# LayerNorm's reciprocal square root moved from GpSimd to VectorE, in a two-layer decode kernel

## The chip, the cores and the metric

The kernel runs on one core of a Trainium2 chip. The metric is the device time of one execution in microseconds; lower is better. The core has TensorE (matrix products, PE in the profile), VectorE (DVE), ScalarE (ACT), GpSimd (POOL) and SyncE (SP), which here issues the transfers. All of them run their own queue of instructions in order and wait for one another by semaphores.

## What is computed

Two decoder layers for eight sequences (B = 8) with one new token each, with the same weights and caches in both layers. Each layer is an attention block and a small MLP, both behind a LayerNorm without scale or offset:

```python
def _layernorm(x, axis=-1, eps=1e-5):
    m = jnp.mean(x, axis=axis, keepdims=True)
    v = jnp.var(x, axis=axis, keepdims=True)
    return (x - m) / jnp.sqrt(v + eps)

    # _A_ref: B=8, Sq=1, D=512, Hq=32, Hkv=8, Sk=8192, Dh=128
    q = (x @ wq) ...                                   # 512 -> 32 heads of 128
    scores = einsum("bhqd,bhkd->bhqk", q, k) * (Dh ** -0.5)
    o = einsum("bhqk,bhkd->bhqd", softmax(scores), v)
    return o ... @ wo                                  # 4096 -> 512
    # _B_ref: F=1792
    return silu(x @ w1) @ w2

    x = A_x
    x = x + _A_ref(_layernorm(x), A_k_cache, A_v_cache, A_wq, A_wo)
    x = x + _B_ref(_layernorm(x), B_w1, B_w2)
    x = x + _A_ref(_layernorm(x), A_k_cache, A_v_cache, A_wq, A_wo)
    x = x + _B_ref(_layernorm(x), B_w1, B_w2)
```

The K and V caches are 8 x 8 x 8192 x 128 bf16 each, and both layers read all of both, so the kernel is mostly a stream of these caches through the core.

## The kernel before

**Tasks and positions.** A task is one layer, one batch row and one KV head: 128 tasks (`make_tasks`). A task is cut into eight positions; each position is half of a granule of 512 KB, eight chunks of 128 keys. At a position TensorE transposes the eight chunks of K (`emit_t`, L383, three positions ahead), a copy on VectorE or ScalarE brings the result back from PSUM (L391, L389), TensorE makes the scores (`emit_s`, L414) and, twelve positions later, multiplies P by V (`emit_pv`, L464). Softmax of a task takes its four steps at the first four positions of the next task: a maximum on VectorE (L423) and across partitions on GpSimd (L425), the subtraction on VectorE (L432) and the exponential on ScalarE (L439), a sum on VectorE (L444) and across partitions on GpSimd (L447), the reciprocal (L452). `emit_norm` (L478) finishes the head.

**Loads.** SyncE issues all transfers (L296), in an order planned beforehand (`plan_loads`), into an arena of 27 slots of 512 KB. A slot is loaded anew when the products that read it are done. Eighteen granules of K of each batch row stay in their slots from the first layer to the second, so that their K is loaded and transposed once; the other nine slots carry the stream.

**The order of tasks.** For each batch row b: the kept heads of layer 0, then three heads of layer 1 of row b - 1, then three heads of layer 0 of row b + 1, then the kept heads of layer 1 of row b.

**The chain.** Between layer 0's attention of a batch row and its layer 1 stands a chain of twelve stages (`chain_of`): `proj` (output projection and residual), three LayerNorm stages `first`, `second`, `third`, `up`, `silu`, `down`, the three LayerNorm stages again, and `query`. One stage is taken out of the list at each position, behind that position's other work, while the tasks of the neighbouring rows go on. Every engine executes in the order of issue, so where TensorE comes to the project of `up` or `query` (L523) it waits for `xnT`, the normalized row, and what was issued behind it waits too. The whole batch goes through one LayerNorm and `query` at the start, and through one `block_stages` at the end, on eight columns instead of one.

**LayerNorm** (`ln_stages`). x lies transposed, 128 partitions x 4 x n columns. `first`: a sum on VectorE into `s1` (L486) and across partitions on GpSimd into `s1a` (L488). `second`: centring into `xc` (L494), square (L500), sum (L501) on VectorE, the partition sum on GpSimd (L503), then on GpSimd the scaling by 1/D with epsilon (L505) and the power of -0.5 (L507), against a tile `nhalf` that is filled once (L327). `third`: the product of `xc` and `s1a` on VectorE into `xnT` (L511). Each call of `op` makes the instruction wait for the last writers of what it reads and for the readers of what it writes, on the same engine too.

## Time and profile before

| | |
|---|---|
| median of 3 runs | 1486.3 us (1485.43 to 1490.5) |
| the profiled execution: its own time | 1487.09 us |
| its span, first to last instruction | 1485.4 us |
| mean granted TensorE clock | 0.71 |
| instructions in the trace | 56919 |
| read from HBM | 473.44 MB, 319 GB/s over the span |
| GpSimd busy | 134.1 us, 338 instructions |
| VectorE busy | 511.5 us, 1246 instructions |

The profile describes one execution. A line of its groups gives source line, engine, operation, output and input tiles, number of instructions, then busy time and the mean of one, and behind the bar the idle time of the engine just before them with what ended it. "issue" means that the engine waited for nothing that the profile shows. POOLq and SPq are the sequencers of GpSimd and SyncE; an instruction that only they execute does not count as busy time. The row named DMA gives for 40 equal slices of the span the busy share of the 16 DMA engines in tenths. Windows repeat the busy times for chosen stretches, with the granted clock, the share of the DMA engines and GB/s at the end of each line.

### The profile page before, as it was taken

What the parts mean: (1) busy time and instruction counts of PE and PEld (TensorE: products, weight loads), DVE (VectorE), ACT (ScalarE), POOL (GpSimd) and SP (SyncE); (2) the same over time, 40 slices, a digit from 0 to 9 for tenths busy, and PEclk for the clock granted to TensorE, in tenths of its full rate; (3) what the DMA queues carried; (4) which work ended last, traced back from release to release, by engine and by line L of the source; (5) the groups of instructions that cost most, each with busy time, mean ns of one, the idle gap of its engine ahead of it and who ended that gap; (6) DMA issues with size and microseconds to landing.
All of it is one profiled execution on the core that took longest, in us unless ns stands there. A gap on an engine that the chain in (4) does not pass through costs nothing.

```text
span 1485.4 us, 56919 instructions
## 1 busy us (share of the span) xinstructions
PE 1008.5 (68%) x25592; PEld 982.2 (66%) x25592; DVE 511.5 (34%) x1246; ACT 327.6 (22%) x414; POOL 134.1 (9%) x338
## 2 busy tenths in 40 slices
PE   2777478658776677856687476783868667775674
PEld 2777477657776567756687476773867667775663
DVE  1343134324342334423344133431434324342331
ACT  1232013212231212312133121330313212231210
POOL 0100010010000110000100001000100011000011
PEclk6788568757696767856588575975868756796665
DMA  8999399829996599956999569993999839996591
GB/s 352 381 407 366 115 403 408 326 102 402 407 405 251 196 408 407 394 188 240 406 407 387 182 263 407 408 355 133 353 408 407 312 130 402 408 388 259 203 408 66
DMA packets 133984, 477.13 MB, mean 321 GB/s; under 512 B 14176, under 2 KB 20080, under 8 KB 133232
## 3 DMA queue, kind: packets, MB, share of 16 engines
q1 hardware_dynamic: 133744, 473.51, 82.2%
q8 instruction: 203, 3.33, 0.9%
q14 instruction: 37, 0.30, 0.1%
HBM read 473.44 MB, written 0.01 MB: 319 GB/s over the span
## 4 chain that ended last, share of the span: by engine, by line
PE 45%; issue 27%; DMA 22%; DVE 3%; POOL 2%; SPq 1%; POOLq 0%; ACT 0%; DVEq 0%
PE TPp L383 20%; DMA arena<-in_A_k_cache_dram 18%; PE SCp L414 10%; PE OTp L464 9%; PE MISC L523 5%; DMA arena<-in_A_v_cache_dram 3%; DVE arena L391 1%; POOL s1a L507 1%; DMA wq<-in_A_wq_dram 1%; SPq L296 1%; POOL s1a L503 0%; POOL mxa L425 0%; POOL s1a L505 0%; DVE sq L500 0%; DVE s L501 0%
## 5 line engine op out<-in xcount | busy, mean ns | idle before, releaser
L383 PE MATMUL TPp<-ident,arena 128*128 128x128 bf16 x5888 | 561.5, 252 | 102.3 <-DMA arena<-in_A_k_cache_dram 69.6
L383 PEld LDWEIGHTS TPp<-ident,arena 128*128 128x128 bf16 x5888 | 422.7, 113 | 110.4 <-DMA arena<-in_A_k_cache_dram 77.1
L391 DVE COPY arena<-TPp 128x1024 bf16<-128x1024 bf16 x460 | 317.2, 690 | 433.0 <-PE TPp L383 430.3
L389 ACT COPY arena<-TPp 128x1024 bf16<-128x1024 bf16 x276 | 278.6, 1009 | 739.4 <-PE TPp L383 739.3
L414 PE MATMUL SCp<-QT,arena 128*128 128x32 bf16 x8192 | 394.4, 184 | 66.7 <-issue 64.0
L464 PE MATMUL OTp<-P,arena 128*128 128x4 bf16 x8192 | 360.8, 165 | 81.6 <-issue 73.4
L414 PEld LDWEIGHTS SCp<-QT,arena 128*128 128x128 bf16 x8192 | 338.7, 103 | 67.8 <-issue 64.2
L464 PEld LDWEIGHTS OTp<-P,arena 128*128 128x128 bf16 x8192 | 290.9, 100 | 95.2 <-issue 86.2
L439 ACT ACTIVATE P<-SCs 128x256 bf16<-128x256 f32 x128 | 53.4, 417 | 384.6 <-DVE SCs L432 331.5
L425 POOL PARTITION_ALL_REDUCE mxa<-mxp x128 | 47.7, 373 | 738.6 <-DVE mxp L423 666.9
L523 PE MATMUL MISC<-xnT,wq 128*128 128x1 bf16 (+1 forms) x1152 | 32.1, 165 | 92.0 <-DVE xnT L511 92.0
L523 PEld LDWEIGHTS MISC<-xnT,wq 128*128 128x128 bf16 x1152 | 31.4, 104 | 92.7 <-DVE xnT L511 77.3
L432 DVE TENSOR_TENSOR SCs<-SCp,mxa 128x256 f32<-128x256 f32 x128 | 53.9, 421 | 87.2 <-POOL mxa L425 87.2
L447 POOL PARTITION_ALL_REDUCE ssa<-ssm x128 | 55.1, 430 | 265.7 <-DVE ssm L444 253.9
L523 PE MATMUL MISC<-xnT,w 128*128 128x1 bf16 (+1 forms) x504 | 14.9, 166 | 86.2 <-DVE xnT L511 86.2
L523 PEld LDWEIGHTS MISC<-xnT,w 128*128 128x128 bf16 x504 | 14.2, 104 | 86.9 <-DVE xnT L511 80.1
L423 DVE TENSOR_REDUCE mxp<-SCp 128x4 f32<-128x256 f32 x128 | 53.4, 417 | 44.5 <-PE SCp L414 44.5
L511 DVE TENSOR_TENSOR xnT<-xc,s1a 128x4 bf16<-128x4 f32 (+1 forms) x18 | 3.2, 178 | 187.3 <-POOL s1a L507 187.3
L444 DVE TENSOR_REDUCE ssm<-P 128x4 f32<-128x256 bf16 x128 | 53.3, 416 | 41.4 <-ACT P L439 41.4
L478 DVE TENSOR_TENSOR at<-OTp,rcp 128x4 bf16<-128x4 f32 x128 | 20.0, 156 | 61.0 <-PE OTp L464 61.0
L523 PE MATMUL MISC<-at,wo 128*128 128x1 bf16 (+1 forms) x1152 | 32.5, 165 | 12.5 <-issue 12.2
L523 PEld LDWEIGHTS MISC<-at,wo 128*128 128x128 bf16 x1152 | 31.3, 101 | 13.2 <-issue 12.8
(33 smaller groups left out, 111.7 us busy)
## 6 DMA issues: line engine op xcount, KB each, us to landing
arena<-in_A_v_cache_dram SPq DMA_DIRECT2D x512, 512.0 KB, 10.1
arena<-in_A_k_cache_dram SPq DMA_DIRECT2D x368, 512.0 KB, 11.8
wq<-in_A_wq_dram SPq DMA_DIRECT2D x2, 2048.0 KB, 9.3
wo<-in_A_wo_dram SPq DMA_DIRECT2D x1, 4096.0 KB, 27.7
w<-in_B_w_dram SPq DMA_DIRECT2D x2, 1792.0 KB, 23.4
X<-in_A_x_dram SPq DMA_DIRECT2D x1, 8.0 KB
out_dram<-X SPq DMA_DIRECT2D x1, 8.0 KB
```

What stands on the lines that cost most here:

```text
L383: lambda c=c: pe.transpose(tpv[:, c, :], chunk(slot, h * GRP + c), ident[:, :])
L389: op(act, lambda: act.copy(dst, TPp[tb][:, :]), reads=[f"TP{tb}"], writes=[r_half(slot, h)])
L391: op(dve, lambda: dve.tensor_copy(dst, TPp[tb][:, :]), reads=[f"TP{tb}"], writes=[r_half(slot, h)])
L414: lambda c=c, o=o: pe.matmul(SCp[bank][:, o:o + SW], chunk(slot, h * GRP + c), rhs, start=True, stop=True,)
L423: op(dve, lambda: dve.tensor_reduce(mxp[st][:, :], scv, AX.X, ALU.max), reads=[f"SC{bank}"], writes=[f"mxp{st}"])
L425: op(pool, lambda: pool.partition_all_reduce(mxa[st][:, :], mxp[st][:, :], 128, bass.bass_isa.ReduceOp.max), reads=[f"mxp{st}"], writes=[f ...
L432: lambda: dve.tensor_tensor(SCs[:, :].rearrange("p (c h) -> p c h", h=REP), SCp[bank][:, 0:NCH * REP].rearrange("p (c h) -> p c h", h=REP) ...
L439: op(act, lambda: act.activation(Ps[pb][:, :], SCs[:, :], ACT.Exp, scale=SM_SCALE), reads=["SCs"], writes=[f"P{pb}"])
L444: op(dve, lambda: dve.tensor_reduce(ssm[st][:, :], Ps[pb][:, :].rearrange("p (c h) -> p h c", h=REP), AX.X, ALU.add), reads=[f"P{pb}"], wr ...
L447: op(pool, lambda: pool.partition_all_reduce(ssa[st][:, :], ssm[st][:, :], 128, bass.bass_isa.ReduceOp.add), reads=[f"ssm{st}"], writes=[f ...
L464: lambda c=c, cc=cc: pe.matmul(otp, chunk(slot, h * GRP + c), Ps[pb][:, cc * REP:(cc + 1) * REP], start=(cc == 0), stop=(cc == NCH - 1),)
L523: lambda o=o, k=k: pe.matmul(MISC[:, o * n:(o + 1) * n], w_sb[:, k, o * 128:(o + 1) * 128], rhs_of(k), start=(k == 0), stop=(k == kparts - 1),
```

## The change

The two GpSimd operations behind the second partition sum and the tile `nhalf` go. `third` computes 1/sqrt(v) on VectorE instead, ahead of the product: v = s1a/D + eps into a tile `vr`; a first guess y from the bits of v, read as an integer (shift right by one, times -1, plus the constant 0x5F3759DF); three Newton steps y = y (1.5 - 0.5 v y y), each in three operations over the tiles `tr` and `yr`. That is twelve operations on n columns. GpSimd keeps the memsets and the mask at the start, and the partition sums and maxima.

```diff
+RSQRT_SEED = float(0x5F3759DF)
+NEWTON = 3
...
-    nhalf = sb([128, B], FP32, "nhalf")
+    vr = sb([128, B], FP32, "vr")
+    yr = sb([128, B], FP32, "yr")
+    tr = sb([128, B], FP32, "tr")
...
-            op(pool, lambda: pool.memset(nhalf[:, :], -0.5), writes=["nhalf"])
...
                     op(pool, lambda: pool.partition_all_reduce(s1a[:, 0:n], s1[:, 0:n], 128, bass.bass_isa.ReduceOp.add),
                        reads=["s1"], writes=["s1a"])
-                    op(pool, lambda: pool.tensor_scalar(s1a[:, 0:n], s1a[:, 0:n], 1.0 / D, LN_EPS, op0=ALU.mult, op1=ALU.add),
-                       reads=["s1a"], writes=["s1a"])
-                    op(pool, lambda: pool.tensor_tensor(s1a[:, 0:n], s1a[:, 0:n], nhalf[:, 0:n], ALU.pow),
-                       reads=["s1a", "nhalf"], writes=["s1a"])
-
                 def third():
+                    v, y, t = vr[:, 0:n], yr[:, 0:n], tr[:, 0:n]
+                    vi, yi = v.bitcast(INT32), y.bitcast(INT32)
+                    op(dve, lambda: dve.tensor_scalar(v, s1a[:, 0:n], 1.0 / D, LN_EPS, op0=ALU.mult, op1=ALU.add),
+                       reads=["s1a"], writes=["vr"])
+                    op(dve, lambda: dve.tensor_scalar(yi, vi, 1, None, op0=ALU.logical_shift_right),
+                       reads=["vr"], writes=["yr"])
+                    op(dve, lambda: dve.tensor_scalar(yi, yi, -1.0, RSQRT_SEED, op0=ALU.mult, op1=ALU.add),
+                       reads=["yr"], writes=["yr"])
+                    for _n in range(NEWTON):
+                        op(dve, lambda: dve.tensor_tensor(t, y, y, ALU.mult), reads=["yr"], writes=["tr"])
+                        op(dve, lambda: dve.scalar_tensor_tensor(t, t, -0.5, v, op0=ALU.mult, op1=ALU.mult),
+                           reads=["tr", "vr"], writes=["tr"])
+                        op(dve, lambda: dve.scalar_tensor_tensor(y, t, 1.5, y, op0=ALU.add, op1=ALU.mult),
+                           reads=["tr", "yr"], writes=["yr"])
                     op(dve, lambda: dve.tensor_tensor(
-                        xnv, xcv, s1a[:, 0:n].unsqueeze(1).to_broadcast([128, KT, n]), ALU.mult),
-                       reads=["xc", "s1a"], writes=["xnT"])
+                        xnv, xcv, y.unsqueeze(1).to_broadcast([128, KT, n]), ALU.mult),
+                       reads=["xc", "yr"], writes=["xnT"])
```

More of the change, by code (lines that the diff above doesn't have):

```diff
@@ L27 @@
 FP32 = mybir.dt.float32
+INT32 = mybir.dt.int32
 ACT = mybir.ActivationFunctionType
```

## The prediction, made before the changed kernel ran

> **What bounds the kernel now.** I read the page first, then the waits, then the two GpSimd lines by source, then one stretch in order of time, and the same stretch in windows. From the page:

> ```profile
> PE 1008.5 (68%) x25592; PEld 982.2 (66%) x25592; DVE 511.5 (34%) x1246; ACT 327.6 (22%) x414; POOL 134.1 (9%) x338
> ...
> DMA  8999399829996599956999569993999839996591
> ...
> L511 DVE TENSOR_TENSOR xnT<-xc,s1a 128x4 bf16<-128x4 f32 (+1 forms) x18 | 3.2, 178 | 187.3 <-POOL s1a L507 187.3
> ```

> No compute engine is full (PE busy 68% of the span, the others less), while most slices of the DMA row stand at 9: there the loads of K and V set the pace, at 405 to 410 GB/s by the windows. The eight dips are the matter. Adding up, over windows of 10 us, what each falls short of 408 GB/s gives 310 us of lost transfer time: 262 in the dips (32.8 each), 26 after the last load, 5 at the start, the rest scattered. The dips are the eight chains (`proj`, LayerNorm, MLP, LayerNorm, `query`), one per batch row. The third line says what happens there: VectorE waits 187.3 us for the power on GpSimd, in 18 LayerNorms. The waits name the next in line and the source:

> ```profile
> PE MISC L523 <- DVE xnT L511: 178.2, 18, 15.4
> ...
> POOL s1a L505 <- issue: 173.5, 18, 10.9
> ...
> POOL mxa L425 <- issue: 71.7, 12, 6.3
> ...
> PE MISC L523 <- DVE hsT L557: 32.9, 9, 4.0
> ```

> (Columns: total us, times, longest.) TensorE stands behind `xnT` for 178.2 us. GpSimd itself waits for nothing that the profile shows ("issue"), 173.5 us ahead of L505. The lines by source show an instruction that the program does not write:

> ```profile
> L505 POOLq MODIFY_POOL_CONFIG  x36: 83/83/88, 27.3 to 1467.5; - x36
> ```
> ```profile
> L425 POOLq MODIFY_POOL_CONFIG  x34: 11/11/11, 40.4 to 1390.2; - x34
> ```

> Two for each of the 18 LayerNorms where GpSimd goes from a partition reduction to ordinary arithmetic, and two for each of 17 ways back. The 256 softmax reductions that follow one another carry none. So it is the alternation that costs, some 10 us out and 6 us back. One chain, in order of time (start, duration, engine, line; in brackets idle time before and its releaser):

> ```profile
> 643.79 0.17 DVE L500 TENSOR_TENSOR sq<-xc 128x4 f32<-128x4 f32 x1
> 643.99 0.16 DVE L501 TENSOR_REDUCE s<-sq 128x1 f32<-128x4 f32 x1
> ...
> 644.25 0.39 POOL L503 PARTITION_ALL_REDUCE s1a<-s  x1 [1.29 <-DVE s L501]
> ...
> 654.42 0.18 POOL L505 TENSOR_SCALAR s1a<-s1a 128x1 f32<-128x1 f32 x1 [9.79 <-issue]
> 654.68 0.60 POOL L507 TENSOR_TENSOR s1a<-s1a,nhalf 128x1 f32<-128x1 f32 x1
> 655.31 0.18 DVE L511 TENSOR_TENSOR xnT<-xc,s1a 128x4 bf16<-128x4 f32 x1 [10.83 <-POOL s1a L507]
> ...
> 655.54 1.65 PE L523 MATMUL MISC<-xnT,w 128*128 128x1 bf16 x56 [9.96 <-DVE xnT L511]
> ...
> 661.22 0.39 POOL L425 PARTITION_ALL_REDUCE mxa<-mxp  x1 [5.94 <-issue]
> ...
> 663.65 1.65 PE L523 MATMUL MISC<-hsT,w 128*128 128x1 bf16 x56 [3.90 <-DVE hsT L557]
> ```

> In windows of the same stretch (PE, PEld, DVE, ACT, POOL busy; then clock, DMA share, GB/s):

> ```profile
> 650.00:660.00 10.00, 4.21 (x104) 4.13 (x104) 0.77 (x2) 0.00 (x0) 0.78 (x2) 0.50 0.05 20
> ...
> 670.00:680.00 10.00, 0.00 (x0) 0.00 (x0) 0.00 (x0) 0.00 (x0) 0.78 (x2) 0.60 0.48 183
> ...
> 690.00:700.00 10.00, 7.72 (x198) 7.37 (x196) 5.08 (x12) 3.34 (x4) 0.80 (x2) 0.97 1.00 379
> ```

> With TensorE standing, no arena slot comes free, the loads in flight run out, and transfers stop: 20 GB/s. Ten microseconds of GpSimd become lost load time.

> **The change, part by part.** *Removed: two GpSimd operations, and with them the alternation.* [...] `up` waits now 86.2 us in nine, of which 11.5 in the tail: 74.7/8 = 9.34 a chain. `query` waits 92.0 in nine, 15.4 at the start: 76.6/8 = 9.58.

> *Added: twelve VectorE operations ahead of `xnT`,* each on one column (eight at both ends of the kernel). None of them is in this trace. The nearest rows are sq and s above: 0.17 and 0.16 us, 0.20 from start to start, each waiting for the one before, as the new ones do. The bounds are 0.155 (the shortest mean of a small VectorE row) and 0.31 (the reciprocal, L556). I take 0.20, since the tiles are as small as those of the nearest rows: 12 x 0.20 = 2.4 us. They begin when the second reduction ends, at 644.64; `xnT` is there at 644.7 + 2.4 + 0.18 = 647.3, and TensorE, which had ended its groups at 645.58, waits 1.8. In `query` a VectorE copy ends first, at 669.39: 669.39 + 2.4 + 0.25 = 672.0 against 669.97, a wait of 2.05. So per chain 9.34 - 1.8 + 9.58 - 2.05 = 15.1 us less. Queued behind the twelve on VectorE are the copies of transposed K, the subtraction and the sums of softmax; TensorE would need them only after the project that it is waiting to start, so they add nothing of their own.

> *The way back goes too.* At 661.22 a softmax maximum waited for GpSimd; behind it in order stood the subtraction on VectorE, then its exponential and the MLP's on ScalarE, then `hsT`, and `down` on TensorE. Of 32.9 us, 1.9 are the tail: 31.0/8 = 3.88 a chain. Without it `up` ends at 647.33 + 1.65 = 648.98, the exponential and three VectorE operations (0.18 + 0.20 + 0.34 + 0.18) give `hsT` by 649.9, and TensorE comes to `down` two positions of 1.28 later, 651.5. I take 0 left. Sum: 15.1 + 3.88 = 18.95 us per chain, and 8 x 18.95 = 151.6. Does a microsecond of TensorE bring one of the end? The dip loses 32.8 us of transfers, more than what is given back, and both sides of it run at the full rate; so yes.

> *What comes to light.* In the busy stretches TensorE stops by itself: between 718 and 818 us its "issue" gaps end 6.1 to 6.7 us apart, 126 matmuls each. With every gap the instruction queue moves one 16 KB packet. `query` alone has 128 matmuls, issued in 3.57 us; today the wait ahead of it hides that. If the next packet comes late, a gap like the 2.24 us in `proj` (ended at 639.91) appears: at most 8 x 2.24 = 18 us, at least 0. Transfers are thin there, so I take 5.

> *The ends.* In the last LayerNorm nothing lies beside the chain: from the end of the reduction (1467.54) to `xnT` (1476.58) 9.04 us; afterwards 12 x 0.23, the pitch of the eight-column rows there, and 0.05: 2.8. Gain 6.2. At the start the first `xnT` comes some 10 us earlier, but transfers then run at 407 GB/s until 50 us; only 2.3 us are missing between 50 and 70, so 0 to 2.3, taken as 1. The dropped memset runs at 0.8 us, beside the load of x: nothing.

> The profiled execution took 1487.1 us (span 1485.4), 0.8 above the median. 1487.1 - 151.6 - 6.2 - 1 + 5 = 1333; on the median, 1332.

> [...] Going to ordinary arithmetic took 9.8 to 10.9 us in the chains and 7.0 in the tail, with no transfers about. [...]

> A second row concerns the short waits that remain:

> ```profile
> 756.82 0.61 PE L383 MATMUL TPp<-ident,arena 128*128 128x128 bf16 x8
> ...
> 761.71 1.01 PE L383 MATMUL TPp<-ident,arena 128*128 128x128 bf16 x8
> ```

> Between them TensorE stood for 2.20 us, and the granted clock fell from 1.00 to 0.50 for the next 5.3. After a gap of 1.88 (at 753.0) it stayed at 1.00, after one of 1.85 (at 772.8) it fell to 0.51. So waits of 1.8 and 2.05 may go either way; I keep positions in the chain at 1.28 us, as now. Were the clock up for six of them, at 0.85 us, 6 x 0.43 x 8 = 21 us more would be won.
> [...]

> **The rivals.** [...] 4%. [...]
> *The loads hide it:* only the tail is won, 1481. Against: transfers are at 20 GB/s in the wait itself. 2%.
> *TensorE's instructions become the bound:* two gaps of 2.24 us a chain instead of the 5 us in all: 1333 - 5 + 36 = 1364. The regular gaps speak for it, the thin transfers against. 14%.
> *The clock stays up:* 1333 - 21 = 1312. 14%.
> *The whole dip closes:* 1487 - 262 - 6 = 1219. Against: a chain's own 368 matmuls still take 10.4 us. 3%.

> **How the numbers follow.** The forecast keeps 63%. VectorE's pitch moves it by 16 x 12 x (-0.045 to +0.11) = -9 to +21, gaps by -5 to +13, the clock by -21, the start by 1: 1297 to 1368. I give 1297 to 1370, which takes in the third and fourth rivals. About 0.3%, 4.5 us, is what a measurement can tell from no change: faster 0.95, same 0.01, slower 0.04.

> **What would show it.** MODIFY_POOL_CONFIG only at the start; no "issue" ahead of L425; TensorE's waits for `xnT` near 40 us instead of 178, for `hsT` under 5; dips of some 14 us instead of 32.8; VectorE up by 216 operations and about 35 us. It is wrong if the dips keep their depth, if the twelve take over 4 us, or if new "issue" gaps stand in `query`.

## The result, and the profile after

The changed kernel takes 1329.1 us (median of four, 1323.6 to 1332.0) against 1485.9 before: a ratio of 0.894, 95% interval 0.890 to 0.897, 156.8 us less. The forecast was 1332, between 1297 and 1370. On another chip the same kernel gave 1328.8 us and 0.893 (0.890 to 0.896). The profiled execution took 1323.6 us (span 1321.8), the fastest of its four; with the 1487.1 of before, the two profiles are 163.5 us apart, and the sums below go by that.

In the page of the changed kernel VectorE has 216 instructions more and 34 us more of work, GpSimd 37 fewer, and the row of transfers has lost its deep dips:

```profile
PE 1009.8 (76%) x25592; PEld 983.4 (74%) x25592; DVE 545.3 (41%) x1462; ACT 328.8 (25%) x414; POOL 117.8 (9%) x301
...
DMA  8999899969999799997999889997999979999892
```

In full windows of 10 us, what is missing from 408 GB/s adds up to 150.6 us instead of 310.6. Each of the eight dips now loses some 15 us of transfers, against some 34 before when both are counted by the windows under 398 GB/s. Its waits (total us, times, longest) answer those of before line by line:

```profile
DVE SCs L436 <- POOL mxa L429: 39.7, 80, 0.5
...
PE MISC L536 <- DVE xnT L524: 36.6, 18, 5.0
...
PE MISC L536 <- issue: 13.2, 9, 2.5
...
PE MISC L536 <- DVE hsT L570: 1.9, 1, 1.9
```

TensorE waits 36.6 us for `xnT` (178.2 before) and 1.9 for `hsT` (32.9 before), while its wait for K from memory stays (70.8 us, 69.6 before) and its own work too (1009.8 us busy, 1008.5 before); "issue" ahead of a partition reduction is gone, and no wait of the subtraction for a maximum is longer than 0.5 us (6.2 before). By source, MODIFY_POOL_CONFIG is left at two places, both in the first 10 us (before the mask and before the first reduction, where the kernel before has it too), and in no chain:

```profile
L335 POOLq MODIFY_POOL_CONFIG  x2: 11/11/11, 1.0 to 1.0; - x2
```
```profile
L492 POOLq MODIFY_POOL_CONFIG  x2: 1/1/1, 9.9 to 9.9; - x2
```

One chain in order of time, to be laid beside that of the prediction:

```profile
588.80 0.40 POOL L507 PARTITION_ALL_REDUCE s1a<-s  x1 [1.28 <-DVE s L505]
...
589.13 0.42 POOL L429 PARTITION_ALL_REDUCE mxa<-mxp  x1
589.23 0.15 DVE L512 TENSOR_SCALAR vr<-s1a 128x1 f32<-128x1 f32 x1 [0.19 <-POOL s1a L507]
589.42 0.15 DVE L514 TENSOR_SCALAR yr<-vr 128x1 int32<-128x1 int32 x1
...
591.35 0.16 DVE L522 SCALAR_TENSOR_TENSOR yr<-tr,yr 128x1 f32<-128x1 f32 x1
591.54 0.18 DVE L524 TENSOR_TENSOR xnT<-xc,yr 128x4 bf16<-128x4 f32 x1
...
591.77 1.62 PE L536 MATMUL MISC<-xnT,w 128*128 128x1 bf16 x56 [1.75 <-DVE xnT L524]
...
595.82 1.63 PE L536 MATMUL MISC<-hsT,w 128*128 128x1 bf16 x56
...
604.07 3.45 PE L536 MATMUL MISC<-xnT,wq 128*128 128x1 bf16 x128 [1.50 <-DVE xnT L524]
```

From the end of the second reduction to `xnT` it is 2.3 us, where it was 10.7. The softmax maximum follows the reduction at once, `down` has no wait left, and from the project of `up` to that of `query` it is 12.3 us, where it was 24.7.

### The profile page after: what moved, and what is told of

It is laid out like the page before. It is cut to its first block, busy times and chain, and to the rows that moved or that the text cites. A ratio compares the mean times of both kernels' runs of the same rounds, so it can differ in the third digit from the quotient of the medians.

```text
span 1321.8 us, 57028 instructions
## 1 busy us (share of the span) xinstructions
PE 1009.8 (76%) x25592; PEld 983.4 (74%) x25592; DVE 545.3 (41%) x1462; ACT 328.8 (25%) x414; POOL 117.8 (9%) x301
## 4 chain that ended last, share of the span: by engine, by line
PE 53%; DMA 23%; issue 17%; DVE 5%; SPq 1%; POOL 1%; ACT 0%; POOLq 0%; DVEq 0%; ACTq 0%
PE TPp L387 24%; DMA arena<-in_A_k_cache_dram 18%; PE SCp L418 12%; PE OTp L468 11%; PE MISC L536 7%; DMA arena<-in_A_v_cache_dram 3%; SPq L301 1%; DVE arena L395 1%; DMA wq<-in_A_wq_dram 1%; DVE yr L522 1%; DVE tr L520 1%; DVE tr L519 1%; POOL s1a L507 0%; DVE xnT L524 0%; DVE yr L514 0%
## 5 line engine op out<-in xcount | busy, mean ns | idle before, releaser
L387 PE MATMUL TPp<-ident,arena 128*128 128x128 bf16 x5888 | 564.0, 253 | 109.2 <-DMA arena<-in_A_k_cache_dram 70.8
L456 DVE RECIPROCAL rcp<-ssa 128x4 f32<-128x4 f32 x128 | 22.0, 172 | 22.8 <-POOL ssa L451 22.8
L536 PE MATMUL MISC<-xnT,w 128*128 128x1 bf16 (+1 forms) x504 | 14.6, 165 | 18.4 <-DVE xnT L524 18.4
```

What stands on the lines that cost most here:

```text
L387: lambda c=c: pe.transpose(tpv[:, c, :], chunk(slot, h * GRP + c), ident[:, :])
L536: lambda o=o, k=k: pe.matmul(MISC[:, o * n:(o + 1) * n], w_sb[:, k, o * 128:(o + 1) * 128], rhs_of(k), start=(k == 0), stop=(k == kparts - 1),
```

## The experiments

The theory of the prediction: GpSimd's change between partition reductions and ordinary arithmetic (the exchange, below) is what costs; it stops TensorE, and so the loads; the twelve VectorE operations cost what they lengthen TensorE's wait. Rivals: that the power itself was slow; that only the reader of `s1a` suffers; that VectorE's work is hidden, or costs by its place in VectorE's queue. Ratios are to the kernel before on the same chip.

**One scaling back on GpSimd.** The eleven other operations stay on VectorE and read `s1a`.

```diff
 # end of second()
+op(pool, lambda: pool.tensor_scalar(s1a[:, 0:n], s1a[:, 0:n], 1.0 / D, LN_EPS, op0=ALU.mult, op1=ALU.add), ...)
 # start of third()
-op(dve, lambda: dve.tensor_scalar(v, s1a[:, 0:n], 1.0 / D, LN_EPS, op0=ALU.mult, op1=ALU.add), ...)
```

> The scaling by 1/D with epsilon goes back to GpSimd, right behind the second partition sum; the other eleven VectorE operations stay, the power is gone. [...] Against the kernel before, eleven operations at 0.195 us (2.15) stand where the power and its gap (0.66) stood, 1.5 us in each of 17 LayerNorms: 1486 + 25 = 1511, between 1490 and 1525, with the waits of TensorE for xnT above 178 us again and 36 and 34 MODIFY_POOL_CONFIG. Rival (the arithmetic itself was slow on GpSimd, the power above all): one operation of 0.18 us per LayerNorm is added to the changed kernel and one of VectorE goes, 1329.

Measured: 1494.7 us, ratio 1.004 (1.003 to 1.005). One operation of 0.18 us brings back the whole loss, and MODIFY_POOL_CONFIG stands in the chains again, 36 times ahead of it and 34 on the way back; the power's own 0.6 us was a trifle. In its waits:

```profile
PE MISC L537 <- DVE xnT L525: 199.0, 18, 15.5
...
PE MISC L537 <- DVE hsT L571: 17.4, 9, 2.2
```

The wait for `xnT` grew by 20.8 us over that of the kernel before, but that for `hsT` fell by 15.5: without the power the way back starts earlier, which the expectation of 1511 had left out. The balance, +5.3 us, is close to the measured step (1494.7 against 1489.5).

**An operation that nobody reads.** The changed kernel, with a scaling of a scratch tile on GpSimd behind each second partition sum (the tile is filled once at the start). `xnT` does not read it; the softmax reductions stand behind it on GpSimd.

```diff
+    dm = sb([128, B], FP32, "dm")
...
 # end of second()
+op(pool, lambda: pool.tensor_scalar(dm[:, 0:n], dm[:, 0:n], 1.0 / D, LN_EPS, op0=ALU.mult, op1=ALU.add), reads=["dm"], writes=["dm"])
```

> The changed kernel, and behind each second partition sum one GpSimd scaling of a scratch tile that nobody reads; all else as in the changed kernel. [...] Theory: out (10) and back (6) hold the softmax maximum for some 16 us; in up's stretch the subtraction, the exponential and hsT stand behind it, and down waits some 11 us; behind query P comes some 5 us too late for its products. 8 x (11 + 5) = 128, 1329 + 128 = 1457, between 1410 and 1475; waits for xnT near 37 us, for hsT near 90. Rival (only who reads GpSimd's arithmetic is held up): 1329 to 1335.

Measured: 1477.9 us, ratio 0.992 (0.990 to 0.994), just above the stated range, 149 us above the changed kernel. Its waits:

```profile
POOL dm L511 <- issue: 170.2, 18, 10.9
...
POOL mxa L431 <- issue: 127.2, 17, 10.6
...
PE MISC L541 <- DVE hsT L575: 88.7, 9, 12.3
...
PE OTp L470 <- ACT P L445: 65.6, 10, 10.9
...
PE MISC L541 <- DVE xnT L529: 34.0, 18, 5.0
```

A way back behind a `query`:

```profile
862.27 0.39 POOL L431 PARTITION_ALL_REDUCE mxa<-mxp  x1 [8.93 <-issue]
```

`xnT` is as early as in the changed kernel, and still almost all the gain is lost: the exchange out and back holds the softmax maxima behind it, some 16 us in the stretch of `up` and some 18 in that of `query`, then VectorE's subtraction, ScalarE's exponential, `hsT` and P. The wait for `hsT` came as expected (some 11 us a chain), that for P was 8 and not 5: in the chains the ways back took 6.0 to 6.2 us behind `up`, but 6.8 to 9.4 behind `query`, where the expectation had 6 for both. So LayerNorm's own wait was only one of two ways to lose the same time.

**The kernel before, with room in the chain.** Eight empty stages between `second` and `third`, for the power to end unseen.

```diff
+EMPTY = 8
...
-                return [first, second, third]
+                return [first, second] + [lambda: None] * EMPTY + [third]
```

> The kernel before, with its scaling and power on GpSimd, and eight empty stages between second and third, some 10 us of TensorE's work, so that s1a is ready when third comes. If only xnT's lateness counted (rival), the 151 us of waits in the chains would be covered: 1489 - 151 = 1338. Theory (the exchange of code also holds the softmax reductions behind it on GpSimd, and with them VectorE's queue, P and TensorE): as in the kernel with an operation that nobody reads, most of the time stays: 1478, between 1440 and 1490, with waits for xnT under 40 us and new ones for P.

Measured: 1501.3 us, ratio 1.009 (1.006 to 1.012), no gain at all. That is above the expected range, which ended at 1490, but the rival's 1338 is far off:

```profile
PE OTp L465 <- ACT P L440: 183.0, 16, 17.3
...
PE MISC L524 <- DVE xnT L512: 48.1, 6, 15.0
```

The waits for `xnT` fell from 178.2 to 48.1 us (what is left stands mainly at the start, in the tail and in the `query` of the first and the last chain) and came back as 183.0 us for P, some 11 us in each of 16. This room in the chain could not do what the change did, since softmax stands in the same GpSimd queue; other orders were not tried.

**Six steps and one step.** `NEWTON = 6` and `NEWTON = 1` (the latter with a coarser root).

> Six Newton steps instead of three: nine more VectorE operations of 0.195 us from start to start, 1.75 us per LayerNorm. Theory (what is left of the waits is the twelve operations, all on TensorE's path, and each microsecond of TensorE's wait in a chain is one of the end): 16 x 1.75 + 1.8 in the tail = 30 us, 1329 + 30 = 1359, waits for xnT 36.6 + 30 = 67 us. Rival (VectorE's work lies beside the loads): 1329 to 1333.

> One Newton step instead of three, six VectorE operations fewer, so a coarser reciprocal root: 1.17 us per LayerNorm less. TensorE's waits of 1.7 in up and 1.65 in query stay above zero (0.5), so the theory gives 16 x 1.17 + 1.2 = 20 us less, 1309; waits for xnT 37 - 20 = 17 us. Rival (VectorE's work lies beside the loads): 1325 to 1329.

Measured: 1352.7 us (ratio 0.908, 0.907 to 0.910) and 1312.2 us (0.880, 0.879 to 0.882); the expectations were 1359 and 1309. The waits for `xnT` with six steps, then with one (67 and 17 us expected):

```profile
PE MISC L536 <- DVE xnT L524: 67.4, 18, 6.8
```
```profile
PE MISC L536 <- DVE xnT L524: 14.4, 14, 3.8
```

So VectorE's work lies on the path, but 53.0 us of waits moved the end by 40.5: not one for one. TensorE's own gaps ("issue"), added over its lines, account for nearly all of the rest: 178.3 us with six steps, 189.8 with one (two executions of the changed kernel itself have 174.9 and 179.0).

**The changed kernel again, and with two empty stages.** The first only as a measure for its neighbours.

```diff
+EMPTY = 2
...
-                return [proj] + ln_stages(x1, r1, n) + [up, silu, down]
+                return [proj] + ln_stages(x1, r1, n) + [lambda: None] * EMPTY + [up, silu, down]
...
-                st += ln_stages(xs[2], "XT2", 1)
+                st += ln_stages(xs[2], "XT2", 1) + [lambda: None] * EMPTY
```

> The changed kernel, unaltered, on the chip of the three kernels beside it, since its executions lay between 1323.6 and 1332.0. 1323 to 1332; it is the measure for the next two.

> The changed kernel with two empty stages in the chain between third and its reader (up, query), so that TensorE does two more positions of the neighbouring rows before it needs xnT. No operation is added or taken away. Theory (the twelve operations cost only by TensorE's wait of 1.7 and 1.65 us in a chain, and two positions of 1.28 us cover that): of 36.6 us of waits for xnT the 5 at the start and the 4.9 in the tail stay, 26.8 go. Six and one Newton steps moved the time by 0.76 of what they moved the waits, so 20 to 27 us: 1302 to 1309, less what new gaps in TensorE's own instruction stream take, up to 8. I expect 1306. Rival (the twelve operations delay the copies of transposed K and the softmax on VectorE, and the end by that): the waits go and the time stays at 1325 or more.

Measured: 1328.8 us (0.893), and 1318.9 us (0.887, 0.884 to 0.891) with empty stages: faster, but by 9.9 and not by the 20 or more expected. Neither the theory nor its rival (1325 or more) has it. Its waits:

```profile
PE TPp L388 <- issue: 34.1, 30, 2.6
...
PE MISC L537 <- issue: 21.2, 13, 2.7
PE MISC L537 <- DVE xnT L525: 18.4, 7, 5.0
```

The waits fell by 17.9 us (36.3 to 18.4; in the last chain there is no room for empty stages). But the gaps rose: over all of TensorE's lines "issue" went from 179.0 to 204.6 us, 25.6 more, where I had allowed 8. TensorE's standing as a whole did not shrink, 309.8 to 313.8 us. What shrank is TensorE's own busy time, 1007.2 to 999.7 us. First the page of the changed kernel, then that with empty stages:

```profile
PE 1007.2 (76%) x25592; PEld 980.8 (74%) x25592; DVE 545.3 (41%) x1462; ACT 329.0 (25%) x414; POOL 117.8 (9%) x301
```
```profile
PE 999.7 (76%) x25592; PEld 972.4 (74%) x25592; DVE 543.4 (41%) x1462; ACT 328.7 (25%) x414; POOL 117.7 (9%) x301
```

The same matmuls ran at a mean granted clock of 0.748 instead of 0.740. Why it was higher is not shown, and the two profiled executions are only 4.1 us apart where the medians are 9.9 apart.

**Fewer steps with and without empty stages.** Two steps with two empty stages, two steps alone, two steps with one empty stage.

> As the kernel with two empty stages, and two Newton steps instead of three. Theory: the chains' waits are covered already, so three operations fewer are worth only what lies bare, the tail's LayerNorm (0.6 us) and the last chain, which has no room for its empty stages before its row's second layer begins: 1 to 2 us below the kernel with two empty stages, 1304. Rival (VectorE's work still counts everywhere): 16 x 0.58 = 9 us below it.

> Two Newton steps instead of three and no empty stages: 0.58 us less in each of TensorE's waits of 1.7 and 1.65 us and in the tail, 9.9 us of waits in all, so 36.6 - 9.9 = 27 us of waits for xnT. If the time follows by 0.76, as between one and six steps, 1329 - 7.5 = 1321; if new gaps in TensorE's own instruction stream take half, 1324. Rival (three VectorE operations fewer are worth 5 us even where empty stages cover them, as the two kernels with empty stages stood, so VectorE's queue counts by itself): 1316.

> Two Newton steps and one empty stage in place of two: the waits left by two steps, 1.1 us, are shorter than one position of 1.28, so one empty stage should cover them as two do, and the chain ends two positions earlier. Theory: waits for xnT 15 to 18 us, as with two empty stages, and the same time, 1314 (1308 to 1318). Rival (the second empty stage was worth something, or cost something): outside that.

Measured: 1313.6 us (0.883, 0.879 to 0.887), 1318.8 us (0.885, 0.883 to 0.887) and 1312.0 us (0.881, 0.879 to 0.882). Two steps alone had waits of 25.2 us for `xnT` (27 expected). Their 1318.8 us lie between the theory's 1321 and the rival's 1316, but on a chip where the kernel before took 1491.2; as ratios these values are about 0.888 and 0.884, so the measured 0.885 stands with the rival, as far as ratios carry over from chip to chip. One empty stage does as well as two, with 16.0 us, as expected. Three operations fewer were worth 5.3 us under empty stages by the medians, more than the 1 to 2 expected; the executions of these kernels spread over 7 to 8 us and their intervals overlap, so how much of it VectorE's queue costs by itself stays open. The last kernel is faster than the change as it was made (0.881 against 0.893) and than two steps alone (0.885), the intervals apart; its interval overlaps that of two steps with two empty stages.

## Why the prediction was right, step by step

**TensorE's waits.** From the two profiles, `up` and its like without the tail went from 74.7 to 13.6 us, 61.1 less (60.3 forecast); `query` without the start from 76.6 to 13.2, 63.4 less (60.2); `hsT` 31.0 less (31.0). Together 155.5 against 151.6. The pitch of the twelve was 0.19 us (0.20 taken), the waits left 1.7 and 1.65 us (1.8 and 2.05).

**The ends.** The tail gave 6.6 us (6.2): from the reduction to `xnT` 2.45 us instead of 9.04, since the pitch there was 0.20 us and not 0.23. The start gave nothing (1 taken): TensorE waits there 5.0 us for `xnT` instead of 15.4, but the first `proj` begins at 136.7 us, 136.5 before, with transfers at 395 GB/s on the mean from 40 to 136 us.

**What did not come.** The 5 us for new gaps in TensorE's stream were not needed: "issue" there is 174.9 us in all, 180.7 before, and none of it stands in `query`. The step was right in kind and too early: the gaps came once the waits were shortened further, 11 to 15 us more with one step and 26 with two empty stages, where one of 0.81 us stands inside a `query` (at 605.45). In sum 155.5 + 6.6 = 162.1, and the profiles are 163.5 apart. The sum on paper was 153.8; the medians, 156.8 apart, lie nearer to it than the profile does, which is the scatter of 8 us among the changed kernel's executions and no better working.

**A microsecond of wait is one of the end.** This held for large steps. TensorE's standing, all its waits added, against the time of the same profiled execution, with TensorE's busy time from the page:

| kernel | TensorE stands, us | time, us | difference | TensorE busy, us |
|---|---|---|---|---|
| before | 472.4 | 1487.1 | 1014.7 | 1008.5 |
| changed | 306.5 | 1323.6 | 1017.1 | 1009.8 |
| scaling on GpSimd | 475.0 | 1493.1 | 1018.1 | 1011.5 |
| unread operation | 448.0 | 1476.0 | 1028.0 | 1021.4 |
| before, eight empty stages | 484.0 | 1501.7 | 1017.7 | 1011.0 |
| six steps | 334.1 | 1352.2 | 1018.1 | 1011.0 |
| one step | 299.1 | 1313.3 | 1014.2 | 1007.4 |
| changed again | 309.8 | 1324.2 | 1014.4 | 1007.2 |
| two empty stages | 313.8 | 1320.1 | 1006.3 | 999.7 |

The difference is in every row the busy time and 6 to 7 us more, so the columns must add up and prove no cause by themselves. What they show is that the waits taken away by the change did not come back: standing fell by 165.9 us and the busy time stayed within 1.3. For small steps a wait taken away came back in part as a gap of TensorE's own (17.9 us of waits against 25.6 us of gaps with two empty stages), and the busy time moved by as much as was at stake (7.5 us there).

**The clock** could be left alone in the chains: from 580 to 610 us it was granted at 0.66, 0.61 and 0.67, against 0.67, 0.50, 0.57, 0.60 and 0.54 from 640 to 690 before, and the groups behind each wait still ran slowly (1.01 us for a transposition group at 593.26). Its mean rose from 0.710 to 0.739.

**The rivals.** The exchange belongs to the arithmetic and not to LayerNorm's reductions: with the arithmetic gone, no MODIFY_POOL_CONFIG stands in the chains, and one operation brings back 36 of them on the way out and 34 on the way back. The loads did not hide the gain. What the prediction saw but priced only inside the chain was the second way of the loss, over softmax; the kernel with the unread operation shows that it is enough by itself to cost 149 us. The two ways lie side by side and their costs do not add.

**The length of the exchange.** In the chains of the kernel before, the way back took 5.8 to 6.3 us with transfers beside it at 3 to 19 GB/s, and the way out 8.5 to 10.6 us (the prediction has 9.8 to 10.9) with 196 to 238 GB/s. At the start the way out took 10.9 us with 408 GB/s, in the tail 7.0 us with none. Of these ways out the one with no transfers beside it is the shortest and the one with the most the longest. With the unread operation the longest way back was 10.6 us, with eight empty stages before `third` the longest way out 12.6; no run changed the transfers alone. That code is exchanged, as the expectation for the eight empty stages has it, no run shows: the traces show two MODIFY_POOL_CONFIG of 83 to 88 ns each on the way out or 11 ns on the way back, then the idle time, and in the 7.0 us of the tail not one packet on any queue.

## What to carry to other kernels

Where one engine alternates between two kinds of work, look at the idle time named "issue" ahead of its instructions and at its sequencer's own entries: one operation of 0.2 us cost two exchanges of 16 to 18 us together, and cost them even when nobody read its result, because the softmax queued behind it waited. Moving a short serial computation to the engine that is already in the chain is priced by operations times pitch (here 12 x 0.19 us), and that against the wait of the engine that sets the end. When the waits of the binding engine have become short, ask what stands right behind them before counting the last microseconds: with two empty stages 17.9 us of waits went and 25.6 us of gaps in TensorE's own stream came.

## What was not expected of the hardware

**A wait for the mask at the start.** In the changed kernel the mask at the start waits 8.2 us, which it did not before:

```profile
9.19 0.28 POOL L335 TENSOR_SCALAR_AFFINE_SELECT ident<-ident 128x128 bf16<-128x128 bf16 x1 [8.20 <-issue]
```

In the kernel with the scaling back on GpSimd, whose last GpSimd instruction is ordinary arithmetic, the same line has no such wait:

```profile
1.28 0.29 POOL L335 TENSOR_SCALAR_AFFINE_SELECT ident<-ident 128x128 bf16<-128x128 bf16 x1 [0.29 <-POOL ident L332]
```

Two MODIFY_POOL_CONFIG stand ahead of the mask in the changed kernel (at 1.0 us) and in the kernel before (at 1.2 and 1.3 us), where the mask at 1.33 us waits 0.30. The wait, 7.9 to 8.7 us, stood in all kernels whose last GpSimd instruction is a partition reduction, and in none where it is arithmetic (0.3 us there). Only this correlation is shown, not its cause, and the kernels that end on a reduction are also those without arithmetic in their chains. It costs nothing here: TensorE starts its first transpositions at 9.6 us instead of 4.8, but then waits 7.1 us for K where it waited 12.0, and the first `proj` stands where it stood before.
